# An attention and MLP kernel rewritten: 32-row score tiles, some exps as VectorE bit copies, Gelu on ScalarE, an issue order from a model

## The chip, the cores and the metric

The kernel runs on one core of a Trainium2 chip. Times are device microseconds (us) of one execution. A core has a matrix engine (PE), VectorE (DVE), ScalarE (ACT), GpSimd (POOL) and SyncE (SP), which here only issues transfers. Each runs its own instructions in order and waits for others by semaphores.

## The reference, cut to what matters

```python
x = A_x                                     # 1 x 2048 x 512, bf16
g = sigmoid((x * gate_w).sum(-1))           # one gate per row
# A: attention, 32 heads of 16, no mask
q, k, v = split(x @ wqkv)
p = softmax(q @ k.T * 0.25)                 # 32 x 2048 x 2048 exps
a = concat_heads(p @ v) @ wo
# B: a mixer and an MLP
h  = gelu(layernorm(x) @ w1)                # 2048 x 512, tanh form
x1 = x + shifted(h) @ w2                    # quarters of the columns shifted by 1, -1, 2, -2 rows
b  = x1 + gelu(layernorm(x1) @ w3) @ w4     # 2048 x 1792 gelus
return g * a + (1 - g) * b
```

The 134 million exps weigh most. ACT works on 128 partitions at once, so it needs over a million columns of exp.

## The kernel before

Each head uses 16 rows of contraction. The kernel before pads q to a full 128-row operand that is zero outside one head, so a score matmul has 128 rows of which 16 matter:

```python
qTs = [qkpool.tile([P, S], BF16, tag=f"qT{h}") for h in range(4)]   # memset to 0, then 16 rows each
def stage_mm(c, kt, p):
    stage = psA.tile([P, 1024], F32, tag="stage")                   # psA has 2 buffers
    for j in range(2):
        nc.tensor.matmul(stage[:, j*512:(j+1)*512], lhsT=kT[:, kt*P:(kt+1)*P],
                         rhs=qTs[2*p+j][:, c*512:(c+1)*512], start=True, stop=True)
...
nc.scalar.activation(out=pt[:], in_=stages[e][:], func=ACT.Exp, scale=0.25)      # L331, 128 x 1024
mlp_tick()                                            # a slice of the MLP every few exps
...                                                   # L341: PV, four heads on four 32-column tiles
nc.tensor.matmul(acc[32*hp:32*hp+DH+1, :], lhsT=vp_g[:, kt, hp, :], rhs=..., tile_position=(0, 32*hp))
```

Gelu is five VectorE steps around a Tanh, which comes from the same ACT table as Exp. The softmax denominators are inverted as 128x512 tiles.

The softmax here doesn't subtract the row's maximum and nothing guards it: scores larger than these inputs give would overflow.

## Time and profile before

| | before |
|---|---|
| time, median | 1226.95 us (1225.97 to 1227.94, 2 runs) |
| PE, ACT, DVE, POOL busy | 1119, 1015, 595, 91 us |
| first exp starts, last exp ends | 53.7, 1183.7 us |
| mean granted PE clock | 0.993 |

The windows view, of the middle of the run (busy time and number of instructions of PE, weight loads, DVE, ACT and POOL, then granted clock, DMA share and GB/s):

```profile
150.00:1050.00 900.00, 861.19 (x4354) 282.07 (x4438) 449.61 (x771) 806.48 (x879) 57.03 (x55) 1.00 0.01 4
```

The timeline of PE (start, duration, engine and line). A listed matmul overlaps the next, so what counts is start to start:

```profile
520.91 0.38 PE L312 MATMUL stage<-qT_3125,kT 128*128 128x512 bf16 x1 [0.52 <-ACT pt L331]
...
521.12 0.38 PE L312 MATMUL stage<-qT_3126,kT 128*128 128x512 bf16 x1
...
521.43 0.39 PE L341 MATMUL acc<-pt,vp_g 128*17 128x512 bf16 x2
...
521.82 0.38 PE L312 MATMUL stage<-qT_3123,kT 128*128 128x512 bf16 x1
```

A score matmul takes 0.21 us, and a group of PV matmuls (two here, as in most groups of this trace) with the mode changes on both sides about 0.48 us (521.34, where the second score matmul has streamed, to 521.82). A mode is the way in which the array is divided into tiles; PV and scores use different ones. PE and ACT are both near their limits and wait for each other through two score buffers.

### The profile page before, as it was taken

The page shows a single profiled execution, that of the slowest core. Times are in us where ns is not written, and L with a number is a line of the kernel's source. Part 1 is how long each engine was busy: PE and PEld are TensorE (multiplying, and loading weights), DVE is VectorE, ACT ScalarE, POOL GpSimd, SP SyncE. Part 2 cuts the span into 40 slices and gives each one's busy share as a digit, 9 for nine tenths or more (in the row PEclk, how much of TensorE's full clock was granted, in tenths as well). Part 3 has the DMA queues.
Part 4 walks back from the last instruction along what each step waited for, and adds up shares of the span by engine and source line. Part 5 has one row for each costly group of instructions (what it writes and reads, how often), then busy time and mean ns, then how long its engine had stood idle before and what let it go on. Part 6 is the DMA issues. An engine that isn't in the chain of part 4 may idle for free.

```text
span 1224.1 us, 14942 instructions
## 1 busy us (share of the span) xinstructions
PE 1119.2 (91%) x5619; PEld 369.0 (30%) x5728; DVE 595.2 (49%) x1036; ACT 1015.3 (83%) x1104; POOL 91.4 (7%) x96
## 2 busy tenths in 40 slices
PE   0499999999999999999999999999999999999988
PEld 0133323322232222333233233332233222322223
DVE  4677445733375444724457325664227743221127
ACT  0168998899978999788988989899987999899960
POOL 4600002000020002000020000200001000000000
PEclk9899999999999999999999999999999999999989
DMA  9300000000000000000000000000000000001007
GB/s 281 83 1 5 5 5 5 1 5 5 5 6 5 5 5 1 6 5 5 5 5 1 5 5 5 5 6 5 1 5 5 5 5 5 5 1 33 7 6 180
DMA packets 39624, 22.58 MB, mean 18 GB/s; under 512 B 26368, under 2 KB 38528, under 8 KB 39552
## 3 DMA queue, kind: packets, MB, share of 16 engines
q1 hardware_dynamic: 34992, 16.26, 4.9%
q10 hardware_dynamic: 4560, 5.38, 1.4%
q8 instruction: 44, 0.72, 0.2%
q14 instruction: 28, 0.23, 0.1%
HBM read 13.24 MB, written 6.29 MB: 16 GB/s over the span
## 4 chain that ended last, share of the span: by engine, by line
PE 61%; ACT 26%; DVE 5%; issue 4%; SPq 2%; DMA 1%; POOL 0%; ACTq 0%; POOLq 0%
PE stage L312 26%; ACT pt L331 23%; PE acc L341 15%; PE ps L222 5%; PE ps L214 4%; DVE rr L352 2%; SPq L85 2%; ACT th L160 2%; PE aps L377 2%; PE ps L256 2%; PE ps L276 2%; PE ps L198 1%; PE ps L189 1%; PE pt L147 1%; PE bc L286 1%
## 5 line engine op out<-in xcount | busy, mean ns | idle before, releaser
L331 ACT ACTIVATE pt<-stage 128x1024 bf16<-128x1024 f32 x1024 | 979.3, 1049 | 119.1 <-PE stage L312 106.0
L341 PE MATMUL acc<-pt,vp_g 128*17 128x512 bf16 x2048 | 375.5, 384 | 10.3 <-ACT pt L331 0.5
L312 PEld LDWEIGHTS <-kT 128*128 128x128 bf16 x2048 | 179.4, 97 | 247.7 <-issue 187.6
L341 PEld LDWEIGHTS <-vp_g 128*17 128x17 bf16 x2048 | 87.9, 87 | 394.4 <-issue 391.6
L349 DVE COPY accsb<-acc 128x512 f32<-128x512 f32 x32 | 22.0, 688 | 180.5 <-PE acc L341 180.4
L352 DVE RECIPROCAL rr<-accsb 128x512 bf16<-128x512 f32 x32 | 107.3, 3352 | 0.9
L161 DVE SCALAR_TENSOR_TENSOR g2T<-th,yh 128x512 bf16<-128x512 bf16 x56 | 38.3, 689 | 126.2 <-ACT th L160 126.2
L328 POOL MEMSET oTg<- 32x512 bf16 x32 | 16.6, 519 | 858.9 <-DMA oT_dram<-oTg 762.8
L153 DVE TENSOR_SCALAR yh<-ps 128x512 bf16<-128x512 f32 x72 | 49.3, 690 | 50.8 <-PE ps L214 40.6
L256 PE MATMUL ps<-xT,wk_pad 128*128 128x512 bf16 x123 | 34.5, 391 | 39.8 <-POOL wk_pad L96 38.9
L214 PE MATMUL ps<-xnT_cc,w_87 128*128 128x512 bf16 x218 | 65.8, 384 | 0.6 <-issue 0.5
L222 PE MATMUL ps<-w_88,g2T 128*128 128x512 bf16 x215 | 64.2, 383 | 0.7 <-DVE g2T L161 0.3
L224 DVE TENSOR_TENSOR x_sb<-x_sb,ps 128x512 bf16<-128x512 bf16 x16 | 11.0, 688 | 103.8 <-PE ps L222 103.8
L160 ACT ACTIVATE th<-sq 128x512 bf16<-128x512 bf16 x72 | 45.8, 645 | 0.0
L278 DVE CAST vp_g<-ps 128x64 bf16<-128x64 f32 x128 | 25.7, 222 | 26.6 <-PE ps L276 23.3
L276 PE MATMUL ps<-wv,xT 128*128 128x64 bf16 x512 | 30.8, 193 | 1.5 <-DVE qT_290 L266 1.1
L377 PE MATMUL aps<-wo_pad,osb 128*128 128x512 bf16 x125 | 30.5, 402 | 0.6 <-DMA osb<-oT_dram 0.4
L158 DVE TENSOR_TENSOR sq<-sq,yh 128x512 bf16<-128x512 bf16 x72 | 30.1, 424 | 1.8
L155 DVE TENSOR_TENSOR sq<-yh 128x512 bf16<-128x512 bf16 x72 | 30.0, 423 | 1.4
L276 PEld LDWEIGHTS <-xT 128*128 128x128 bf16 x512 | 24.9, 98 | 18.5 <-issue 7.5
L256 PEld LDWEIGHTS <-wk_pad 128*128 128x128 bf16 x128 | 12.7, 100 | 57.2 <-POOL wk_pad L96 41.9
L312 PE MATMUL stage<-qT_1876,kT 128*128 128x512 bf16 x64 | 24.3, 379 | 4.6 <-ACT pt L331 4.1
(278 smaller groups left out, 1285.6 us busy)
## 6 DMA issues: line engine op xcount, KB each, us to landing
oT_dram<-oTg SPq DMA_DIRECT2D x32, 128.0 KB, 1.8
osb<-oT_dram SPq DMA_DIRECT2D x16, 256.0 KB, 3.1
x_sb<-in_A_x_dram SPq DMA_DIRECT2D x1, 2048.0 KB, 18.0
out_dram<-ot SPq DMA_DIRECT2D x16, 128.0 KB, 2.0
w_87<-in_B_w_dram ACTq DMA_DIRECT2D x1, 1792.0 KB, 14.7
w_88<-in_B_w_dram ACTq DMA_DIRECT2D x1, 1792.0 KB, 21.6
wraw<-in_A_wqkv_dram SPq DMA_DIRECT2D x1, 1024.0 KB, 6.6
w_183<-in_B_w_dram ACTq DMA_DIRECT2D x1, 512.0 KB, 22.8
```

Source lines behind the costliest of these rows:

```text
L153: nc.vector.tensor_scalar_mul(out=yh[:], in0=ps[:], scalar1=0.5)
L160: nc.scalar.activation(out=th[:], in_=sq[:], func=ACT.Tanh)
L161: nc.vector.scalar_tensor_tensor(out=dst, in0=th[:], scalar=1.0, in1=yh[:], op0=ALU.add, op1=ALU.mult)
L214: nc.tensor.matmul(ps[:], lhsT=w3[:, kt, mch * P:(mch + 1) * P], rhs=xn2T_cc[:, kt, :], start=(kt == 0), stop=(kt == KT - 1))
L222: nc.tensor.matmul(ps[:], lhsT=g2T[:, k14, j * P:(j + 1) * P], rhs=w4[:, k14, :], start=(k14 == 0), stop=(k14 == FT - 1))
L256: nc.tensor.matmul(ps[:], lhsT=wk_pad[:, kt, g * P:(g + 1) * P], rhs=xT[:, kt, c * 512:(c + 1) * 512], start=(kt == 0), stop=(kt == KT - 1))
L276: nc.tensor.matmul(ps[:], lhsT=xT[:, kt, t * P:(t + 1) * P], rhs=wv[:, kt, 64 * g:64 * (g + 1)], start=(kt == 0), stop=(kt == KT - 1))
L312: nc.tensor.matmul(stage[:, j * 512:(j + 1) * 512], lhsT=kT[:, kt * P:(kt + 1) * P], rhs=qTs[2 * p + j][:, c * 512:(c + 1) * 512], start=T ...
L331: nc.scalar.activation(out=pt[:], in_=stages[e][:], func=ACT.Exp, scale=0.25)
L341: nc.tensor.matmul(acc[32 * hp:32 * hp + DH + 1, :], lhsT=vp_g[:, kt, hp, :], rhs=ptt[:, (hp % 2) * 512:(hp % 2 + 1) * 512], start=(kt == ...
L352: nc.vector.reciprocal(out=rr[:], in_=accsb[:])
L377: nc.tensor.matmul(aps[:], lhsT=osb[:, g, :], rhs=wo_pad[:, g, :], start=(g == 0), stop=(g == NG - 1))
```

## The change

The intent is to relieve both. Score matmuls use 32-row tiles, each holding a pair of heads with one head's q zeroed, so that up to four run at once in the array. A quarter of the exps goes to VectorE: a multiply and add writes 16-bit integers whose bits, read as bf16, are a piecewise-linear exp; shifted copies of them (add 32 to the integer), weighted in V, smooth the error. Gelu becomes ACT's own function. The remaining matmuls are split into four 32-column tiles, so that they share PE's mode with PV. The issue order comes from a small event model of the engines inside the kernel file. The diff, cut to its core (the real one rewrites the file):

```diff
-    nc.tensor.matmul(stage[:, ...], lhsT=kT[:, kt*P:(kt+1)*P], rhs=qTs[2*p+j][:, ...])     # 128 rows
+    nc.tensor.matmul(dst(), lhsT=kT[G][32*i:32*i+32, kt*P:(kt+1)*P],
+                     rhs=qt[G, c][32*i:32*i+32, p, :], tile_position=(32*i, 0))            # L673
-    nc.scalar.activation(out=pt[:], in_=stages[e][:], func=ACT.Exp, scale=0.25)
+    nc.scalar.activation(out=box["p"][:, 0:n], in_=get()[:, 0:n], func=ACT.Exp, scale=0.25)  # L732, n = 1536 or 1024
+    # VectorE's tiles: L769, then copies 1 and 2 (L792); copy 3 on POOL (L795)
+    nc.vector.tensor_scalar(out=d[:, 0, ...], in0=score, scalar1=BITS_MUL, scalar2=BITS_ADD, op0=mult, op1=add)
+    nc.vector.tensor_scalar(out=d[:, k, 0:w], in0=d[:, k-1, 0:w], scalar1=32.0, op0=add)
+    nc.gpsimd.tensor_scalar(out=d[:, 3, 0:w], in0=d[:, 2, 0:w], scalar1=1.0, scalar2=32.0, op0=mult, op1=add)
-    # Gelu: 5 VectorE operations around ACT.Tanh
+    ge.append(act(..., pre + ge, lambda: nc.scalar.activation(..., func=ACT.Gelu_apprx_tanh)))  # four calls in a batch
-    nc.tensor.matmul(ps[:], lhsT=w3[:, kt, mch*P:(mch+1)*P], rhs=xn2T[:, kt, :])
+    for j in range(4):
+        nc.tensor.matmul(ps[32*j:32*j+32, :], lhsT=lf(32*j, 32*j+32), rhs=rf(), tile_position=(0, 32*j))   # L381
+    sim.run(pe_pick, ...); sim.order.sort(); [fn() for _, _, fn in sim.order]    # issue order from the model
```

## The prediction

> **What bounds it now.** Two engines in lock step. In the page's chain PE has 61%, ACT 26%. In the windows view, 150 to 1050 us, PE is busy 861 us, ACT 806, DVE 50%. ACT: 26 back-to-back exps of 1024 columns take 23.94 us in the timeline, 0.92 us each; 1024 of them, 938 us, plus 72 tanh. PE: score matmuls start 0.215 us apart though a head uses 16 of 128 rows; an isolated group of four PV matmuls costs 0.31 us and about 0.09 before it (mode change). Per two exps: 4x0.216 + 0.40 + about 0.5 of projections and MLP = 1.8 us, as much as ACT's 1.84. They wait for each other through two stage buffers: 1.07 us an exp. The exps begin at 54 us and end at 1184: head 54, tail 40.
>
> **The change, counted from its instruction order.** 2048 score tiles of 32 rows (a head pair, one head's q zeroed), up to four at once; ACT exps 1545 tiles in 309 calls of 1536 and 309 of 1024 columns; DVE takes 503 as bit copies.
>
> - ACT: 309x(0.92+1.35) = 701 us (1.35 estimated: 512 more columns at 0.83 ns). Gelu, 36,864 columns in 20 calls: 32 us. Table loads: the order has 41, since exps slip in between almost all Gelu calls of a batch. One lasts 1.283 us in the trace, as in the Trainium skill (ScalarE: Activation LUTs, What ACT_TABLE_LOAD costs): 53 us, 46 more than the change's own model counts. Sum 786.
> - PE: QK falls from 2048x0.216 = 442 us to 551 runs of about 3.7 matmuls. The Trainium skill (TensorE: Matmul & The Clock Gate, Part 3) measured 3.07x for four row tiles; no run here shows it yet. Estimate 0.095 us mode change + 0.28: 210 to 240 us. PV grows (3557 matmuls in fours, 195 us), other work 180, changes back 52. Sum 650 to 720: no longer first.
> - DVE: 503 PSUM passes at 0.60, 504 shifted copies at about 0.34, 152 evacuations and 32 accumulator copies at 0.6 (0.61 pitch in the trace), statistics 25, small 20: about 630 us. POOL about 360 (252 third shifts of 1 us). If they hold each other up at their shared port, DVE might reach 700.
> - Gone: weight padding, 107 us of reciprocals, the DVE Gelu. Head: xT in 16 transposes, 1.85 us each by the 29.66 us for all before; first exp near 16 us. Tail: after the last PV five DMA hops of about 2 us, a multiply, matmul, store: about 17 us.
>
> **Time.** All of ACT's change lies on the path, since ACT becomes the limit. 786/0.92 (8% idle: waits in a fixed issue order with three busy engines) = 854, less some loads that fall into waits, plus head and tail: **865 us**, range 800 to 940. Faster by over 2%: 0.97, within: 0.02, slower: 0.01.
>
> **Right if** ACT is busy 760 to 800 us, about 90% of the span, first in the chain; 41 ACT_TABLE_LOAD; an exp of 1536 listed at about 1.45 us; first exp before 20 us; last exp to end under 22 us; DVE 75 to 85%.
>
> **Wrong if** row tiles do not overlap (QK toward 440 us, PE first, over 950); if DVE and POOL serialise so that ring buffers come late and PE, in fixed order, stalls (900 to 950); if 32-column tiles run slower than wide matmuls; or if ACT idles under 4% (near 810).

## More of the kernel before

The profile page first, parts 1, 2 and 4: busy time of each engine; 40 slices with the busy tenths of each; the chain of work that ended last.

```profile
PE 1119.2 (91%) x5619; PEld 369.0 (30%) x5728; DVE 595.2 (49%) x1036; ACT 1015.3 (83%) x1104; POOL 91.4 (7%) x96
...
ACT  0168998899978999788988989899987999899960
...
PEclk9899999999999999999999999999999999999989
...
PE 61%; ACT 26%; DVE 5%; issue 4%; SPq 2%; DMA 1%; POOL 0%; ACTq 0%; POOLq 0%
```

## The result, and the profile after

957.13 us median (953.41 and 960.85), against 1226.95: the ratio is 0.7803, 95% interval 0.7729 to 0.7877. A ratio here is the mean time of one kernel's fast runs over that of the other's of the same rounds, so it is not quite the ratio of the medians. The change is a large gain, but the time lies above the predicted range of 800 to 940.

The page of the kernel after, the same lines:

```profile
PE 832.3 (87%) x8949; PEld 258.6 (27%) x8949; DVE 715.2 (75%) x1338; ACT 807.8 (85%) x680; POOL 386.9 (41%) x405
...
ACT  0665999999889999998979899799998889999990
...
PEclk9997999998799999976979997999968999969996
...
PE 51%; ACT 16%; DVE 16%; issue 8%; DMA 3%; SPq 3%; POOL 2%; ACTq 0%; POOLq 0%; DVEq 0%
```

ACT's busy time is near what was predicted (786), but PE's granted clock has holes: its mean is 0.921. The clock records of this trace hold only full and half, so half-clock time is 2 x (1 - 0.921) x 951.6 = 150 us; before it was 17. The groups by form (count, busy us, mean ns of one, idle before):

```profile
L732 ACT ACTIVATE PA<-psA 128x1536 bf16<-128x1536 f32 x309 | 452.5, 1464 | 75.4 <-PE psA L673 62.4 <-PE acc L820 9.0 <-PE ring L673 1.9
...
L732 ACT ACTIVATE PA<-psA 128x1024 bf16<-128x1024 f32 x309 | 320.7, 1038 | 31.7 <-PE acc L820 17.9 <-PE psA L673 10.8 <-PE ring L673 1.9
...
L795 POOL TENSOR_SCALAR PD<-PD 128x1024 uint16<-128x1024 uint16 x251 | 263.0, 1048 | 466.3 <-DVE PD L792 300.9 <-PE ring L673 58.4 <-PE psA L673 44.7
L792 DVE TENSOR_SCALAR PD<-PD 128x1024 uint16<-128x1024 uint16 x502 | 252.3, 503 | 10.6
...
L732 ACT ACT_TABLE_LOAD x21 | 26.9, 1283 | 11.3 <-DMA wq<-in_A_wqkv_dram 11.0
...
L600 ACT ACT_TABLE_LOAD x16 | 20.5, 1283 | 0.3
```

With four more loads at the first Gelu batch that is 41, 53 us of ACT. The middle of the run in the windows view:

```profile
100.00:900.00 800.00, 725.11 (x7916) 223.75 (x7913) 630.61 (x1178) 731.06 (x615) 336.99 (x338) 0.93 0.10 26
```

ACT is busy 731 of 800 us, so idle 8.6%, close to the 8% of the prediction. ACT's timeline through one Gelu batch with PE's pause in it, and what the windows view says of the time before, within and after it:

```profile
409.51 1.28 ACT L600 ACT_TABLE_LOAD   x1
410.81 1.91 ACT L600 ACTIVATE h<-h 128x2048 bf16<-128x2048 bf16 x1
412.74 1.28 ACT L732 ACT_TABLE_LOAD   x1
414.03 1.02 ACT L732 ACTIVATE PA<-psA 128x1024 bf16<-128x1024 f32 x1
415.07 1.28 ACT L600 ACT_TABLE_LOAD   x1
...
415.11 0.56 PE L673 MATMUL psA<-q,kT 32*128 32x512 bf16 x2 [3.21 <-ACT PA L732]
```

```profile
403.00:415.00 12.00, 8.68 (x92) 2.50 (x93) 9.44 (x18) 11.94 (x10) 4.80 (x5) 1.00 0.17 40
415.00:446.00 31.00, 25.00 (x134) 4.52 (x133) 16.13 (x31) 27.25 (x22) 8.56 (x9) 0.50 0.06 16
446.00:476.00 30.00, 27.74 (x257) 7.36 (x255) 27.72 (x51) 28.63 (x25) 13.67 (x14) 1.00 0.05 13
```

A batch of four Gelu calls keeps ACT from its exps for 409.5 to 430.3, with three exps between. PE stands still for 3.2 us of it, its clock falls to half at 415, and it stays there until 446. In that stretch PE gets through 134 matmuls, against 257 in the next 30 us. (Half of the stretch is still the batch; from its end at 430.3 to 445.9 the same view has 81 in 15.6 us.) The same happens near 240, 580, 710 and 840 us.

The start is slower than predicted too. Pieces of the chain in order of time (start, us, what):

```profile
18.96 1.26 SPq L351
20.27 2.81 DMA xT<-in_A_x_dram
...
68.07 11.46 DMA zE_dram<-zE
...
81.40 1.59 DMA pk<-den
```

The first exp begins at 24.3 us, after the last of the 16 transposes (line 351) although its own inputs are there by about 13 us. At 68 us the gate values go to DRAM as 2048 single 4-byte elements, which takes 11.5 us in place of the modelled 2.2. The softmax transfers of the first round stand behind it, VectorE's next instruction in order waits for them, and ACT has a gap of 9.6 us (78.1 to 87.7).

### The profile page after: what moved, and what is told of

It is laid out like the page before. It is cut to its first block, busy times and chain, and to the rows that moved or that the text cites. A ratio compares the mean times of both kernels' runs of the same rounds, so it can differ in the third digit from the quotient of the medians.

```text
span 951.6 us, 22237 instructions
## 1 busy us (share of the span) xinstructions
PE 832.3 (87%) x8949; PEld 258.6 (27%) x8949; DVE 715.2 (75%) x1338; ACT 807.8 (85%) x680; POOL 386.9 (41%) x405
## 4 chain that ended last, share of the span: by engine, by line
PE 51%; ACT 16%; DVE 16%; issue 8%; DMA 3%; SPq 3%; POOL 2%; ACTq 0%; POOLq 0%; DVEq 0%
PE acc L820 17%; PE ring L381 15%; PE psA L673 12%; ACT PA L732 10%; DVE PD L769 7%; PE ring L673 6%; DVE PD L792 5%; ACT L732 3%; SPq L351 2%; ACT L600 2%; DMA zE_dram<-zE 1%; DVE st L483 1%; ACT h L600 1%; POOL PD L795 1%; DVE accsb L836 1%
## 5 line engine op out<-in xcount | busy, mean ns | idle before, releaser
L732 ACT ACTIVATE PA<-psA 128x1536 bf16<-128x1536 f32 x618 | 720.1, 1251 | 107.1 <-PE psA L673 73.3
L795 POOL TENSOR_SCALAR PD<-PD 128x1024 uint16<-128x1024 uint16 x252 | 263.6, 1046 | 466.7 <-DVE PD L792 300.9
L769 DVE TENSOR_SCALAR PD<-ring 128x512 uint16<-128x512 f32 x503 | 338.0, 683 | 146.9 <-PE ring L673 120.0
L820 PE MATMUL acc<-PD,V 128*17 128x512 bf16 x2012 | 309.6, 408 | 14.4 <-POOL PD L795 6.3
L673 PE MATMUL psA<-q,kT 32*128 32x512 bf16 x1545 | 247.7, 397 | 53.0 <-ACT PA L732 51.2
L820 PE MATMUL acc<-PA,V 128*17 128x512 bf16 x1545 | 266.9, 396 | 3.0 <-DVE V L446 1.2
L792 DVE TENSOR_SCALAR PD<-PD 128x1024 uint16<-128x1024 uint16 x504 | 253.6, 504 | 10.6
L673 PE MATMUL ring<-q,kT 32*128 32x512 bf16 x503 | 185.4, 403 | 15.2 <-DVE kT L406 8.6
L820 PEld LDWEIGHTS <-V 128*17 128x17 bf16 x3557 | 91.9, 90 | 248.1 <-issue 211.7
L381 PE MATMUL ring<-xnT,w 128*32 128x512 bf16 x1152 | 86.5, 381 | 0.5 <-DVE PD L769 0.2
L732 ACT ACT_TABLE_LOAD x21 | 26.9, 1283 | 11.3 <-DMA wq<-in_A_wqkv_dram 11.0
```

The costliest lines, as they stand in the source:

```text
L381: units.append([Op("col", j, lambda j=j, lf=lf, rf=rf, st=st, sp=sp: nc.tensor.matmul(get()[32 * j:32 * j + 32, 0:N], lhsT=lf(32 * j, 32 * ...
L673: o = Op("row", i, lambda: nc.tensor.matmul(dst(), lhsT=kT[G][32 * i:32 * i + 32, kt * P:(kt + 1) * P], rhs=qt[G, c][32 * i:32 * i + 32, p ...
L732: nc.scalar.activation(out=box["p"][:, 0:n], in_=get()[:, 0:n], func=ACT.Exp, scale=0.25)
L769: nc.vector.tensor_scalar(out=pr["box"]["d"][:, 0, h * 512:(h + 1) * 512], in0=get()[:], scalar1=BITS_MUL, scalar2=BITS_ADD, op0=ALU.mult, ...
L792: nc.vector.tensor_scalar(out=d[:, k, 0:w], in0=d[:, k - 1, 0:w], scalar1=float(SHIFT), scalar2=None, op0=ALU.add)
L795: nc.gpsimd.tensor_scalar(out=d[:, k, 0:w], in0=d[:, k - 1, 0:w], scalar1=1.0, scalar2=float(SHIFT), op0=ALU.mult, op1=ALU.add)
```

## The experiments

In all but the first the edit is to the changed kernel or to an earlier edit, as said. The results in one table; half-clock time is 2 x (1 - clock) x span of the profiled run.

| run | kernel | median us (range, 4 runs) | ratio to before, 95% | half clock us |
|---|---|---|---|---|
| r0 | changed kernel again | 960.2 (958.0 to 960.6) | 0.7812, 0.7799 to 0.7825 | 175 |
| r1 | Tanh in Gelu's place | 895.3 (894.2 to 897.1) | 0.7292, 0.7281 to 0.7303 | 48 |
| r2 | Gelu contiguous | 932.3 (925.4 to 933.7; a slow run, 945.5) | 0.7576, 0.7543 to 0.7610 | 154 |
| r3 | gate latency in the model | 978.6 (976.3 to 984.1) | 0.7975, 0.7949 to 0.8001 | 205 |
| r4 | transposes in the model | 961.1 (958.1 to 961.9) | 0.7824, 0.7810 to 0.7838 | 196 |
| r5 | wide matmuls | 978.9 (976.6 to 986.4) | 0.7983, 0.7951 to 0.8016 | 181 |
| r6 | no third copy on POOL | 936.7 (935.5 to 941.8) | 0.7643, 0.7619 to 0.7667 | 153 |
| r7 | no exps on VectorE | 1159.3 (1148.9 to 1163.5) | 0.9430, 0.9380 to 0.9480 | 597 |
| r8 | r2 + PE filled in Gelu | 910.0 (904.5 to 917.4) | 0.7417, 0.7375 to 0.7459 | 56 |
| r9 | r2 + start repaired | 926.0 (923.7 to 927.7) | 0.7543, 0.7526 to 0.7559 | 155 |
| r10 | r8 + start repaired | 904.6 (902.0 to 905.2; a slow run, 918.5) | 0.7372, 0.7357 to 0.7387 | 56 |
| r11 | r10 + third copy on VectorE | 897.7 (895.5 to 903.7) | 0.7321, 0.7294 to 0.7348 | 58 |
| r12 | gate in row form only | 955.9 (954.3 to 967.4) | 0.7817, 0.7764 to 0.7869 | 139 |
| r13 | r11 with row-form gate | 897.5 (896.3 to 899.5) | 0.7315, 0.7304 to 0.7327 | 38 |
| r14 | r13, third copy on POOL | 912.8 (909.7 to 920.1) | 0.7447, 0.7412 to 0.7482 | 86 |
| r15 | true arrival times only | 969.9 (964.9 to 974.4) | 0.7902, 0.7864 to 0.7941 | 216 |
| r16 | r13, fewer PV matmuls | 908.2 (902.2 to 911.9) | 0.7391, 0.7355 to 0.7427 | 103 |
| r17 | r13, row strips chosen | 900.6 (898.8 to 901.6) | 0.7334, 0.7322 to 0.7347 | 34 |

One warning for reading it: any edit that changes the model's numbers changes the whole issue order, and r3 and r15, which only correct the model, came out 18 and 10 us slower than the control. Differences of up to some 20 us between different orders are therefore not evidence of one cause by themselves. Runs r1 and r6 keep the order of the changed kernel, and r16 that of r13.

### r0 to r3: the loads, and the gate transfer

> The changed kernel again, unaltered, as the control for the runs beside it: 950 to 962 us, ACT busy about 808 us, 41 table loads, mean granted clock about 0.91 to 0.92, first exp at 24 us.

```diff
 # r1: both Gelu lines; wrong result on purpose (relative error 0.036)
-    func=ACT.Gelu_apprx_tanh
+    func=ACT.Tanh
```

> Gelu replaced by Tanh in the same place, issue order untouched; wrong result on purpose. Tanh shares exp's table, so 40 of 41 table loads (51 us of ACT) go. Theory L (table loads lie on the critical path, because ACT is the limit): 51 us less, and up to 15 us more where the granted clock no longer falls, so 885 to 905 us, clock above 0.96. Rival P (PE, DVE and POOL set the pace and the loads fall into waits): less than 20 us gained, above 935 us.

```diff
 # r2: one job for a batch, so the model cannot put an exp between
-    for q, (a, b) in enumerate(((0, 4), (4, 8), (8, 11), (11, 14))):
-        ge.append(act(93 + 427*(b-a) + (1300 if q == 0 else 0), pre + ge, lambda: activation(h[:, a:b], Gelu)))
+    def gelu_2():
+        for a, b in ((0, 4), (4, 8), (8, 11), (11, 14)): activation(h[:, a:b], Gelu)
+    ge.append(act(4*93 + 427*FT + 2*1300, pre, gelu_2, prio=0))       # and the same for the first Gelu
```

> The Gelu calls of a batch issued as one block, so that no exp slips between them: 11 table loads in place of 41, 38 us less of ACT. Theory L: 910 to 925 us, and half-clock time down by more than half since ACT is away for 9 us in place of 20. Rival P: above 940 us. If the pause of 9 us still lets the PE clock fall, half-clock time stays above 100 us.

```diff
 # r3
-    d1 = dma(2200.0, [a], lambda: nc.sync.dma_start(out=zE_dram..., in_=zE[:]))
+    d1 = dma(12000.0, [a], lambda: nc.sync.dma_start(out=zE_dram..., in_=zE[:]))
```

> Only the modelled latency of the small gate transfer to DRAM is changed, from 2.2 to 12 us (the trace has 11.5), so that the transfers and VectorE steps behind it are ordered later. Theory Q (that transfer holds the in-order DMA queue, then DVE at a reciprocal, then PE and ACT): the 9.6 us gap of ACT near 78 us and the half clock after it disappear, 8 to 14 us less, 940 to 948 us. Rival: the gap is hidden elsewhere by slack later, no change within 3 us.

r1 gained 65 us with the order untouched. The first line of the page's part 1 in r0, r1, r2 and, for later, r8:

```profile
PE 841.8 (88%) x8949; PEld 259.0 (27%) x8949; DVE 716.8 (75%) x1338; ACT 808.2 (84%) x680; POOL 386.7 (40%) x405
PE 807.3 (90%) x8949; PEld 255.1 (29%) x8949; DVE 717.6 (80%) x1338; ACT 751.6 (84%) x640; POOL 387.8 (43%) x405
PE 845.8 (91%) x8961; PEld 253.0 (27%) x8961; DVE 716.0 (77%) x1346; ACT 766.2 (82%) x649; POOL 389.7 (42%) x407
PE 818.1 (91%) x9333; PEld 258.5 (29%) x9333; DVE 710.3 (79%) x1330; ACT 766.9 (85%) x652; POOL 385.2 (43%) x404
```

ACT's busy time fell from 808.2 to 751.6 us, by 56.6, and ACT was idle some 8 us less. That is not all the loads' own time: half-clock time fell with them, from 175 to 48 us, and r1 alone does not part the two (the table after r8 does). r2 removed 30 of the 41 loads (ACT busy 766.2, 42 us less) and gained only 28 us, less than expected, and its half-clock time hardly fell. The reason is in ACT's and PE's record around a batch. r2's windows, from where the clock falls:

```profile
410.80:444.90 34.10, 33.82 (x193) 5.53 (x196) 21.22 (x40) 23.96 (x21) 11.97 (x13) 0.50 0.04 11
444.90:475.00 30.10, 27.62 (x280) 7.81 (x276) 26.88 (x51) 28.54 (x26) 13.94 (x14) 1.00 0.08 22
```

The contiguous batch (400.9 to 410.0 with its two loads) is pause enough for the clock to fall. At half clock PE is busy 99% of the stretch and ACT 70% (23.96 of 34.1 us), after it ACT is busy 95%. So in this stretch, at half clock, PE is the limit.

r3 missed: it was slower. The pause stayed (a gap of ACT of 7.1 us), because the round's first transfer (den<-accsb, 8 KB) still stood behind the gate transfer in the transfer queues and took 10.6 us itself. Ordering the waiting instructions later does not help when the transfer itself holds the queue. Why the rest of the run became slower was not settled.

### r4 to r7: undoing parts

```diff
 # r4: each transpose holds the queue 1.3 us
-    j_xT[c, k] = dma(2600.0 + 300.0 * k, [], ...)
+    j_xT[c, k] = xdma(2800.0, [], ...)                    # hold 1300 in place of 60
 # r5
-    COL = True
+    COL = False
 # r6: copy 3 not made, its PV reads copy 2; wrong on purpose, though still inside the tolerance
-    nc.gpsimd.tensor_scalar(out=d[:, 3, 0:w], in0=d[:, 2, 0:w], ...)
 # r7
-    DVE_STOP, DVE_ALONE, SLACK = 6, 0, 120.0
+    DVE_STOP, DVE_ALONE, SLACK = 64, 0, 120.0
```

> Only the modelled arrival of the 16 x transposes is changed (1.3 us each, one after another, 2.8 us to landing, as the trace has them; the model had them all in by about 4 us), so that the first score matmuls no longer stand behind key projections of later rows. Theory: first exp at 12 to 15 us in place of 24, and since ACT is the limit most of that stays: 8 to 12 us less, about 948 to 952. Rival: the early exps only move a wait, since the first round needs all keys: under 3 us gained.

> The other matmuls undone to wide ones (128 columns, one instruction in place of four 32-column tiles). Theory C (the small tiles pay because they share a mode with PV and save about 0.09 us at each change): PE gets some 300 to 500 more mode changes, PE idle and ACT idle grow, 10 to 40 us slower, 970 to 1000. Rival (fewer instructions are better or equal): 940 to 962.

> The third shifted copy on POOL left out, its PV reading the second copy; wrong result on purpose; same order. Takes 263 us of POOL away. Theory L (ACT is the limit, shared port only a side cost): the mean of VectorE's shifted copies falls from 0.50 us toward 0.35, DVE busy falls by 50 to 80 us, but the time changes by less than 12 us. Rival D (DVE waiting for POOL at the port delays score buffers and so ACT): 25 us or more gained.

> The bit copies on VectorE undone: all 2048 score tiles through ACT's exp. ACT gets 503 more tiles of 0.45 us = 228 us. Theory L: the time grows by nearly that, 1130 to 1200 us, with ACT above 88% busy. Rival P (the pace is set by PE, which is freed of 1509 PV matmuls, and by DVE): under 1080 us.

r4 was a failed edit: the first exp stayed at 24.2 us, since the model's weights queue behind its transposes and so arrived even later. r5: wide matmuls cost 2.2% (0.7983 over 0.7812 is 1.022), in the range expected, and PE's trace has 1377 runs of one mode where r0's has 1107, so 270 more mode changes. But the order is another, and r3 lost as much by that alone: that the small tiles pay is likely, not shown. r6 gained 23 us with the order kept, between the two theories. The copies of VectorE in r0, then in r6:

```profile
L792 DVE TENSOR_SCALAR PD<-PD 128x1024 uint16<-128x1024 uint16 x502 | 253.1, 505 | 10.6
```

```profile
L792 DVE TENSOR_SCALAR PD<-PD 128x1024 uint16<-128x1024 uint16 x502 | 224.8, 449 | 10.6
```

They are 0.056 us shorter each without POOL's work. That POOL and DVE hold each other up here fits the Trainium skill ("SBUF — State Buffer", Who interferes with whom, on the port pair that the two share as an exclusive lock), but even with POOL's copies gone a copy is listed at 0.45 us, not the 0.34 of the prediction (which is what the kernel's own model has, 0.26 ns a column and 72 ns). How much of the 23 us is the port and how much the earlier result for PV, r6 does not separate.

r7: without VectorE's exps the time is 199 us longer, for 220 us more of ACT's busy time (1028.4 against 808.2). In sum the bit copies are worth nearly all of what they take from ACT. But PE, with less to do, is at half clock for 597 of 1162 us, so the 199 us are not ACT's work alone.

### r8 to r11: a fill for PE, and the start

```diff
 # r8 on top of r2: when PE has nothing to do while the model has a Gelu batch on ACT
+    zw = const.tile([P, DH + 1], BF16); memset(zw, 0.0)
+    if not ops: ops = warm_ops()        # 3 groups of 4: acc[32i:32i+17] += zw.T @ xT[:, 0, 0:512], adds zero
 # r9 on top of r2: arrival times, this time with the weights ahead of the transposes, and the gate on ACT's queue
+    dl_w = {"k": Job("SP", 1, 6500.0, [], None, prio=-1), "v": Job("SP", 1, 11000.0, [], None, prio=-1)}
-    d1 = dma(2200.0, [a], lambda: nc.sync.dma_start(out=zE_dram...))
+    d1 = Job("ACT", 400.0, 12000.0, [a], lambda: nc.scalar.dma_start(out=zE_dram...))
 # r10 = r8 + r9; r11 = r10 with copy 3 on nc.vector
```

> Against the contiguous Gelu run (933 us, 154 us at half clock): the same, with idle PE time during each Gelu block filled by matmuls with zero weights that add nothing to the accumulator, so that the PE clock has no pause to fall in. Theory H (the half clock after a Gelu block costs time of its own): half-clock time under 80 us and 10 to 25 us less, 908 to 923. Rival (half clock is harmless because ACT is the limit): clock restored but time within 5 us of 933; or the fill only delays the next score tiles, above 938.

> Contiguous Gelu plus two repairs of the start, no fill: true arrival times of the weights and of the transposed x in the order model (the earlier attempt left the weights behind the transposes, so nothing moved), and the small gate transfer sent from ACT's queue so that the round's own transfers do not stand behind it. First exp at 13 to 16 us in place of 24, no ACT gap above 5 us near 80 us. Theory: both waits lie on the path since ACT is the limit; against 933 us 12 to 20 us less, 912 to 922. Rival: a wait is only moved, above 926.

> Contiguous Gelu, repaired start and PE fill together. If the effects add: 890 to 905 us, ACT busy about 767 us, half clock under 80 us.

> As the run with everything, and the third shifted copy moved from POOL to VectorE. Leaving that copy out gained 23 us. If what it cost was POOL holding the port and its late result: 5 to 15 us less than the run with everything, DVE busy 750 to 790 us. If VectorE's own time matters more: 5 to 20 us slower than it.

r8 is the test of the clock. ACT's busy time is that of r2 (766.9 against 766.2 us), half-clock time falls from 154 to 56 us and the time by about 20 us (0.7576 to 0.7417). The stretch after the same Gelu batch in r8, where the batch ends at 406.7:

```profile
406.00:440.00 34.00, 28.61 (x264) 7.73 (x263) 26.36 (x50) 31.28 (x28) 13.27 (x13) 0.95 0.05 12
```

PE does 264 matmuls, none of them fill, where r2 did 193 in its 34 us at half clock, and ACT is busy 92% where it was 70%. The fill is 396 matmuls that compute nothing. (r2 and r8 ran on different chips; the kernel before agreed within 0.1% on the two.)

r8's order is another than r2's too, so the gain alone would prove little. What the clock costs can be read more directly: ACT's idle time between its first and last exp, split by the granted clock. It is worked out from the clock records and ACT's instructions of each profiled run, in us:

| run | half clock: length | ACT idle in it | full clock: length | ACT idle in it |
|---|---|---|---|---|
| changed kernel, first profile | 133 | 25 | 770 | 72 |
| r0, the same kernel | 160 | 33 | 751 | 71 |
| r1, Tanh | 31 | 16 | 815 | 79 |
| r2, contiguous | 130 | 45 | 752 | 72 |
| r6, no third copy | 140 | 23 | 746 | 60 |
| r8, r2 + fill | 31 | 15 | 823 | 74 |
| r13 | 18 | 6 | 836 | 81 |
| r16 | 89 | 29 | 779 | 71 |

Between r2 and r8 nearly all of the difference is idle time at half clock, 30 us. Between the two profiles of the changed kernel, of one order, the second is 7 us longer and has 8 us more idle time at half clock. r1's 65 us are 57 of busy time and 17 of idle time at half clock, less 8 of idle time at full clock that came back; so about 8 us of the loads had fallen into waits. r2 saved 42 us of busy time and lost 12 of them to idle time at half clock. Not every such us is the clock's doing: 8 of the 25, 33, 16 and 15, and 11 of r2's 45, lie in the pause behind the gate transfer (81 to 91 us in the first profile), where PE waited as well.

r9 brought the first exp to 17.0 us, but the gain against r2, 6 us by the medians, is not clear of noise (the intervals overlap) and below what was expected; the pause near 78 us was still there. In r10's chain:

```profile
64.55 10.20 DMA den<-accsb
74.76 1.79 DMA pk<-den
```

Another queue for the gate transfer did not free the round's transfers. r11 is 7 us faster than r10, in another order, so no evidence by itself.

### r12 to r15: the start by itself

```diff
 # r12: exp(-z) for the normalisation once more, as four rows
+    matmul(ps[32*c:32*c+32, :], lhsT=gw32[:, k, :], rhs=xT[:, k, c*512:(c+1)*512], tile_position=(0, 32*c))   # 16 of them
-    dma_start(out=zE_dram.rearrange("(t p) -> p t"), in_=zE)              # 2048 elements of 4 bytes
+    dma_start(out=zE_dram.rearrange("(c n) -> c n"), in_=zr[0:128:32, :]) # 4 rows of 2 KB
 # r13 = r11 with this in place of the ACT queue; r14 the same with copy 3 on POOL; r15: r9's arrival times alone
```

> The changed kernel with the gate for the normalisation computed a second time by 16 column-tile matmuls in row form, so that it goes to DRAM as four rows of 2 KB in place of 2048 single elements; all else as in the changed kernel. Theory Q: den<-accsb of the first round takes about 2 us in place of 10 to 12, ACT's 9.6 us gap near 78 us goes, and with it the half clock behind it: 8 to 15 us less than 960, 945 to 952. Rival (only moved): 957 to 963.

> Contiguous Gelu, true arrival times, row-form gate, PE fill, third copy on VectorE. If the pause of 10 us near 78 us was on the path: 8 to 12 us less than 898, 884 to 891, and the faster of all runs.

> The same with the third copy left on POOL: 892 to 900 us, 5 to 10 us slower than with VectorE, as in the pair before (905 against 898).

> The changed kernel with the true arrival times alone (weights and transposes): first exp at 17 us in place of 24. If that wait is on the path, 5 to 8 us less than 960; if the first round waits for keys and values anyway, under 3 us.

The pause is gone in r12: ACT's longest gap between 68 and 90 us is 1.1 us, and its idle time between 50 and 100 us is 10.6 us where r0 has 20.3. Yet the ratio cannot be told from that of r0 (0.7817 against 0.7812; r12's interval is 0.7764 to 0.7869, so a gain of some us is not excluded). In the profiled runs about half of what was won was given back: after 100 us ACT is idle 82 us in r12, 77 in r0. Why was not settled. r15 shows the same for the head, the first exp at 17.1 us and a slower run with 216 us of half clock. r13 adds the row-form gate to r11 and gains nothing that can be told from noise, but it is the steadiest fast version: 897.5 us. It beats the kernel before by 27% and the changed kernel by 6% and is correct. r14 against r13 has the third copy on POOL and is 15 us slower, in another order and with 48 us more at half clock.

### r16 and r17: is PE by now an equal limit?

```diff
 # r16 on r13: PV matmuls of copies 3 and 4 not emitted, order kept
-    o = Op("col", i, lambda: nc.tensor.matmul(acc[...], ...))
+    o = Op("col", i, None if drop else lambda: nc.tensor.matmul(acc[...], ...))
 # r17 on r13: VectorE's score tile on a strip i that the other tiles of the run leave free
-    i0 = dcount[0] % 4
+    for i0 in sorted(range(4), key=lambda i: (i in used or ..., drows[i])):
```

> Best version so far (898 us) with the PV matmuls of the third and fourth copy left out at emission, all else and the order unchanged; wrong result on purpose. Takes 988 matmuls, 247 groups of 0.217 us = 54 us, from PE and nothing from ACT. If PE limits together with ACT (fixed order, two score buffers): 20 to 45 us less, 853 to 878. If ACT alone limits: less than 8 us.

> Best version so far with VectorE's score tile chosen on a row strip that the other tiles of the same run do not use; the work is the same. Runs of three or four score tiles without a repeated strip take 0.32 us in place of 0.53, so perhaps 20 to 40 us less of PE time. If PE limits too: 10 to 25 us less, 873 to 888, the fastest of all. If ACT alone limits: within 5 us of 898.

r16 took 988 PV matmuls from PE (an estimate of 54 us, 247 groups of 0.217 us) and was 11 us slower. Half-clock time rose from 38 to 103 us: PE with less work lost its clock more often. By the table above ACT's idle time rose by 23 us at half clock and fell by 9 at full clock. So the amount of PE's work limited r13 by some 9 us at most of the 54, and r16 is no clean test, since its clock changed as well. (Its result was still within the tolerance, so two copies are close enough here; it is no better version, as it was slower.) r17 did make runs of four score tiles shorter: their median time to the next instruction of the other mode fell from 0.53 us in r13 to 0.325. But the order got 592 runs of score tiles in place of 553, each with its mode change, and the sum over PE was the same, so it tests nothing. Its time is 3 us longer.

## Why the prediction was wrong

The direction was right, and so was the mechanism in the main: what ACT has to do sets the time. The time was 92 us too low. The failing step is the closing sum: "786/0.92 (8% idle ...) = 854, less some loads that fall into waits, plus head and tail". It deducted loads that hardly fell into waits, and it had no term for what the loads and gaps do to PE's clock. Its terms, against the profiled run of 951.6 us:

| term | predicted | measured | difference |
|---|---|---|---|
| ACT busy, first to last exp | 786 | 806 | +20 |
| ACT idle there, at full clock | 68 | 72 | +4 |
| ACT idle there, at half clock | no term | 25 | +25 |
| loads that fall into waits | -22 | in the idle time | +22 |
| head and tail | 16 + 17 | 24 + 24 | +15 |

The -22 is what the prediction's deduction amounts to: without it its terms add to 887. The differences add to 86, the measured terms to the profiled span.

- "less some loads that fall into waits" was too hopeful, and the sum lacked the clock. r1, with the order kept, gained 65 us for 51 us of loads: about 8 us of them had fallen into waits, but 17 us of idle time at half clock went with them. r8 shows the same from the other side: the pause around a Gelu batch lets PE's clock fall, and PE at half clock cannot feed ACT. The Trainium skill has a rule ("TensorE: Matmul & The Clock Gate", Part 1, the two states: half clock after an idle window of about 3.4 us). Traces agree only in part. At 415 PE had stood still for 3.2 us; but in the same trace the clock fell at 476.6, and in r2 at 410.8, with no pause of PE over 0.91 us in the 15 us before, PE being listed busy for 71% and 55% of the last 3.4 us. In these two traces only one fall between the first and the last exp has a pause of over 3.4 us in the 15 us before it (4.2 us, before the fall at 241).
- ACT's busy time was 20 us more: the exps took 720 us against 701, since an exp that is followed by a gap or a load is not overlapped by its neighbour (1.46 us listed, 1.34 in a row; 194 of the 618). The count of 41 loads and 53 us was right.
- "8% idle" held in the middle (8.6% from 100 to 900 us), in part by luck, since the prediction reckoned without the half clock and these 800 us hold 120 us of it. In the first 76 us after the first exp ACT was idle 27 us, 9.6 of them behind the gate transfer, which the prediction did not look at.
- "first exp near 16 us": 24.3. The transposes were costed, but not that the fixed order puts the key projections of all rows before the first score tile. r15 shows that mending this alone does not shorten the run, so its part of the miss is bookkeeping more than cause.
- "Right if ACT is first in the chain" failed: PE has 51%, ACT 16%. r7 (220 us more of ACT, 199 us longer) and r16 (54 us less of PE, not faster) say that ACT's work still counted for most, though the half clock rose in both. Of the prediction's other marks, 41 loads, an exp of 1.46 us and DVE at 75% held; ACT's busy time, the first exp and the tail (24 us against under 22) lay outside. The chain names who released last, not whose work is the limit.
- PE: row tiles overlap. By the lower quartile of the time from each run's first matmul to the next run's, at full clock, r0's score runs sum to 240 us (predicted 210 to 240) and all of PE to 716 (650 to 720). The Trainium skill's 3.07x for four row tiles (same page, Part 3) was a fair basis: four tiles on four strips take 0.325 us in r17, with one mode change, where four matmuls of before take 0.86, so 2.6 times; but where two of a run share a strip, the usual case in the changed kernel, it is 0.53.
- DVE: 715 us listed against 630, mainly the shifted copies, 0.50 us each in place of 0.34. The prediction had named this ("if DVE and POOL serialise"). r6, with the order kept, puts POOL's copies and what hangs on them at 23 us, about half of it idle time of ACT at half clock.

What remains open: in r13, at full clock nearly throughout, ACT is still idle 10% between its first and last exp (87 of 854 us). r13's waits there name score tiles (41 us) and the freeing of exp buffers by PV (41 us); neither less PE work nor a better start removed them. That they come from the fixed order with its two score buffers is argued, not shown.

## What to carry to other kernels

Count table loads in the issued order, not in the source: a chain of calls that each wait for the one before leaves gaps into which other functions slip, here 41 loads for 5 batches of Gelu. When one engine pauses for some microseconds, ask what the matrix engine does meanwhile: filling the pause with matmuls that add zero gained about 20 us here. And an order fixed by a model is only as good as its durations, but mending one of them changes the whole order: judge by several runs, and do not count on early gains: r15's was given back whole, r12's in part.

## What the Trainium skill lacked or had wrong

- "ScalarE: Activation LUTs", What ACT_TABLE_LOAD costs: 1283 ns agrees with every load here. The drain of about 1380 ns on top does not show: a load starts 0.02 us after the call before it (409.50 to 409.51), and the next call 0.02 us after the load. All 40 removed loads cost ACT 56.6 us of busy time, 1.4 us each.
- "TensorE: Matmul & The Clock Gate", Part 1: that one busy window of about 3.4 us brings the clock back is not enough here. In r2 PE was busy 99% of 34 us, in small tiles with mode changes, and stayed at half clock all that time. What it takes with 32-row and 32-column tiles, no page says. The idle window of the two states does not describe most falls here either (above). In the traces of r1, r2, r8, r13 and of the changed kernel every stretch at half clock that lies between the first and the last exp lasts a multiple of about 3.4 us, 3.4 to 34.1.
- "TensorEngine Tiling (Array Packing)", Key Properties, says that a mode change drains PE, without a time. Here, from runs of 4 and 8 column tiles that took 0.327 and 0.543 us to the next mode, a change costs about 0.11 us (0.327 less the 0.216 of a group).
- The same page does not say that two tiles of one run on the same row strip go one after the other; here it makes 0.53 us of 0.325.
- "DMA: Bandwidth & Descriptors", Rules for kernel authors, warns that single elements cost one descriptor each, without a time. Here 2048 elements of 4 bytes took 11.5 us, and an 8 KB transfer behind them 10.6 us on the same queue (r3) and 10.2 us on another (r10), against 2.0 us at most where the gate went as four rows (r12), which its section on queues does not lead one to expect.
